# A fused attention and MLP-mixer kernel: hand-set order on every engine, first-batch masks on TensorE, and the next batch's token mix inside the current channel mix

## The chip, the cores and the metric

One core of a Trainium2 chip. The time is the device time of one execution in microseconds (us). The span of a profile is about 2 us shorter than the time of the same run (257.0 against 258.93 us before the change).

Engine names in the profile lines: PE is TensorE's matmul stream, PEld its weight loads, DVE is VectorE, ACT ScalarE, POOL GpSimd, SP SyncE. PSUM is the memory that the matmuls write to; its tiles are named after what they hold: ps_tr transposes of q and k, ps_s scores, ps_o attention output, ps_h `tok1`, ps_u `tok2`, ps_ut transposes of u, ps_v `ch1`, ps_w `ch2`. qb, kb and va are q, k and v cast to bf16, pT the exponentials, x_b the output of attention, u_sb the u of the reference.

## The reference, cut to what matters

```python
q, k, v: (4, 8, 768, 64)            # batch, heads, sequence, head dim; f32
keep = (key < 4) | (0 <= query - key < 128)        # 4 sink keys and a window of 128
x = softmax(where(keep, q @ k.T / 8, -1e9)) @ v    # heads joined: (4, 768, 512)
h = relu(x.T @ w_tok1) @ w_tok2                    # token mix, 768 -> 256 -> 768
u = x + h.T
out = u + relu(u @ w_ch1) @ w_ch2                  # channel mix, 512 -> 1536 -> 512
```

## The kernel before

The work is cut into eight groups of four heads, two groups for each batch. Per group: cast q and k to bf16 and transpose them (`tr`, six 128x128 TensorE transposes each), scores in three units per head pair (`sc`), exponential by ScalarE, masks, products with v (`pv`), normalisation by VectorE. Then per batch: `tok1` twice (once for each group), `tok2` and `utr` (I call `tok2` and `utr` together the *head*), then `ch1` and `ch2`. Attention of the next batch is laid into the channel mix of the current one.

```python
def sc(j, u):                        # cut
    ...
    nc.scalar.activation(pT[:, :, 512*u:512*u+n], ps[:, :, 0:n], AF.Exp, scale=scale)
    if u == 0:
        (nc.vector if fast else nc.gpsimd).tensor_tensor(... mask0 ..., op=ALU.mult)
    if dve_mask: ...                 # group 1, second head pair: VectorE multiplies
    elif u == 2:
        for i in range(2):           # window edges by GpSimd, in place
            nc.gpsimd.affine_select(out=cur, in_=cur, ...)
            nc.gpsimd.affine_select(out=prv, in_=prv, ...)

def tok2(st):
    ps = ps_mx.tile([P, DM], FP32, name="ps_u", tag="mx")    # two buffers, shared with ch1, ch2
    ...
    nc.vector.tensor_tensor(out=u_sb[:, st], in0=ps, in1=x_b[:, st], op=ALU.add)

with tc.manual_schedule(engines={PE}):      # only TensorE in the written order;
    ...                                     # the scheduler orders the other engines
    for b in range(B):
        t1, m = mixers.pop(b)
        main, fill = t1[1] + m, []          # m starts with the head
        ...                                 # attention of b + 1 at 0.03 .. 0.96 of main
        main = main + mixers[b + 1][0][0]   # first tok1 of b + 1
        for f in spread(main, fill):
            f()
```

The softmax here doesn't subtract the row's maximum and nothing guards it: scores larger than these inputs give would overflow.

Of the kernel before, what the change touches and what calls it, by code (L numbers as in the profile page):

```python
# [13 lines left out]
PE = mybir.EngineType.PE  # L14
# [3 lines left out]
def kernel(  # L18
# [45 lines left out]
    maskm = singles.tile([P, 2, P], BF16, name="maskm")  # L64
    warm = singles.tile([P, 512], BF16, name="warm")
    hm = singles.tile([P, 2, 4], BF16, name="hm")
    dm = singles.tile([4 * GH, GH, 1], FP32, name="dm")
    ks = [[singles.tile([P, P], BF16, name=f"ks{a}{j}") for j in range(2)] for a in range(2)]
    vs_c = singles.tile([4 * GH, NG, D], FP32, name="vs_c")
# [13 lines left out]


    def load_qk(g, lo, hi, q32, k32):
        b, h0 = g // GB, GH * (g % GB)
        return [nc.sync.dma_start(
            out=dst[:, lo:hi].rearrange("p h t d -> p h (t d)"),
            in_=src[b, h0 + lo:h0 + hi].rearrange("h (p t) d -> p h (t d)", t=NT))
            for src, dst in ((q, q32), (k, k32))]  # L90

    def load_v(g, v32):
        b, h0 = g // GB, GH * (g % GB)
        return nc.sync.dma_start(out=v32.rearrange("p h t d -> p (h t) d"),
                                 in_=v[b, h0:h0 + GH].rearrange("h (t p) d -> p (h t) d", p=P))

    def stage_tiles():
        return (stage.tile([P, GH, NT, D], FP32, name="q32"),
                stage.tile([P, GH, NT, D], FP32, name="k32"),
                stage.tile([P, GH, NT, D], FP32, name="v32"))  # L100

    def load_group(g, *behind):
        t3 = stage_tiles()
        for d in load_qk(g, 0, GH, t3[0], t3[1]) + [load_v(g, t3[2])]:
            after(d, *behind)
        return t3

    def load_sinks():
        for h in range(GH):
            nc.sync.dma_start(  # L110
                out=vs_c[4 * h:4 * h + 4],
                in_=v.rearrange("b (a h) s d -> h s (b a) d", h=GH)[h, 0:4])

    def load_weights(behind):
        wt1 = moe_w_tok1.rearrange("(t p) n -> p t n", p=P)
        wt2 = moe_w_tok2.rearrange("(t p) n -> p t n", p=P)
        wc1 = moe_w_ch1.rearrange("(t p) n -> p t n", p=P)
        wc2 = moe_w_ch2.rearrange("(t p) n -> p t n", p=P)
        hf = DCH // 2
        after(nc.gpsimd.dma_start(out=w_tok1, in_=wt1), behind)  # L120
        nc.gpsimd.dma_start(out=w_tok2, in_=wt2)
        nc.gpsimd.dma_start(out=w_ch1[:, :, 0:hf], in_=wc1[:, :, 0:hf])
        d = nc.gpsimd.dma_start(out=w_ch1[:, :, hf:DCH], in_=wc1[:, :, hf:DCH])
        nc.gpsimd.dma_start(out=w_ch2[:, 0:NF // 2], in_=wc2[:, 0:NF // 2])
        nc.gpsimd.dma_start(out=w_ch2[:, NF // 2:NF], in_=wc2[:, NF // 2:NF])
        return d

    def build_constants():
        nc.vector.memset(warm, 0.0)
        make_identity(nc, ident)  # L130
        nc.vector.memset(mask0, 1.0)
        nc.gpsimd.affine_select(
            out=mask0[:, :, 0], in_=mask0[:, :, 0], compare_op=ALU.is_ge,
            fill=0.0, base=0, pattern=[[0, 2], [1, P]], channel_multiplier=-1)
        nc.gpsimd.affine_select(
            out=mask0[:, :, 1], in_=mask0[:, :, 1], compare_op=ALU.is_ge,
            fill=0.0, base=-1, pattern=[[0, 2], [-1, P]], channel_multiplier=1)
        nc.vector.tensor_copy(out=maskm, in_=mask0[:, 0])
        nc.vector.memset(mask0[0:4], 1.0)
        nc.vector.memset(hm, 1.0)  # L140
        nc.vector.memset(hm[64:128, 0], 0.0)
        nc.vector.memset(hm[0:64, 1], 0.0)
        for a in range(2):
            for j in range(2):
                nc.gpsimd.memset(ks[a][j], 0.0)
        nc.vector.memset(vsink, 0.0)

    def build_sinks():
        nc.gpsimd.memset(dm, 1.0)
        nc.gpsimd.affine_select(  # L150
            out=dm[:, :, 0], in_=dm[:, :, 0], compare_op=ALU.is_ge, fill=0.0,
            base=0, pattern=[[-4, GH]], channel_multiplier=1)
        nc.gpsimd.affine_select(
            out=dm[:, :, 0], in_=dm[:, :, 0], compare_op=ALU.is_ge, fill=0.0,
            base=3, pattern=[[4, GH]], channel_multiplier=-1)
        for h in range(GH):
            nc.vector.tensor_scalar(
                out=vsink[0:4 * GH, :, h, 0:D], in0=vs_c,
                scalar1=dm[:, h], scalar2=None, op0=ALU.mult)
            nc.vector.tensor_copy(  # L160
                out=vsink[0:4 * GH, :, h, D:D1],
                in_=dm[:, h:h + 1].to_broadcast([4 * GH, NG, 1]))


    class Group:
        pass

    def cast_tiles():
        G = Group()
        G.qb = bfp.tile([P, 2, NT, 2, D], BF16, name="qb")  # L170
        G.kb = bfp.tile([P, 2, NT, 2, D], BF16, name="kb")
        G.va = bfp.tile([P, GH, NT, D1], BF16, name="va")
        G.qT, G.kT, G.pT = [None, None], [None, None], [None, None]
        return G

    def cast_qk(G, j, q32, k32, fast):
        for (src, dst, eng) in ((q32, G.qb, nc.vector), (k32, G.kb, nc.gpsimd)):
            o = dst[:, j].rearrange("p t i d -> p i t d")
            (eng if fast else nc.gpsimd).tensor_copy(out=o, in_=src[:, 2 * j:2 * j + 2])

    def cast_v(G, v32):
        nc.gpsimd.memset(G.va[:, :, :, D:D1], 1.0)
        nc.gpsimd.tensor_copy(out=G.va[:, :, :, 0:D], in_=v32)

    def attention(g, G, x_b, fast):
# [3 lines left out]
        def tr(j, which):  # L189
# [4 lines left out]
            dst = att.tile([P, P, NT], BF16, name="qT" if which == 0 else "kT")  # L194
            view = ps.rearrange("d t p -> d p t")
            if which == 1 and not fast:
                nc.scalar.activation(dst, view, AF.Copy)  # L197
            else:
                nc.vector.tensor_copy(out=dst, in_=view)  # L199
            flat = dst.rearrange("d p t -> d (p t)")  # L200
            if which == 0:
                G.qT[j] = flat
            else:
                G.kT[j] = flat
                nc.gpsimd.tensor_tensor(  # L205
                    out=kz[j][:, 8 * j:8 * j + 8].rearrange("p (i s) -> p i s", i=2),
                    in0=flat[:, 0:4].unsqueeze(1).to_broadcast([P, 2, 4]), in1=hm, op=ALU.mult)

        def sc(j, u):
            dve_mask = g == 1 and j == 1  # L210
# [3 lines left out]
            n = 0  # L214
            for kt in (2 * u, 2 * u + 1):
                w = (2 if kt < NT - 1 else 1) * P
                for i in range(2):
                    nc.tensor.matmul(  # L218
                        ps[:, i, n:n + w],
                        G.kT[j][ds(64 * i, 64), ts(kt, P)], G.qT[j][ds(64 * i, 64), ds(kt * P, w)],  # L220
                        start=True, stop=True)
                n += w
            pT = G.pT[j]
            nc.scalar.activation(pT[:, :, 512 * u:512 * u + n], ps[:, :, 0:n], AF.Exp, scale=scale)  # L224
            if u == 0:
                (nc.vector if fast else nc.gpsimd).tensor_tensor(
                    out=pT[:, :, 0:2 * P], in0=pT[:, :, 0:2 * P],
                    in1=mask0.rearrange("p i c q -> p i (c q)"), op=ALU.mult)
            if dve_mask:
                lo, hi = (2 * P, 4 * P) if u == 0 else (512 * u, 512 * u + n)  # L230
                for x in range(lo, hi, 2 * P):
                    w = min(2 * P, hi - x)
                    nc.vector.tensor_tensor(
                        out=pT[:, :, x:x + w], in0=pT[:, :, x:x + w],
                        in1=maskm.rearrange("p c q -> p (c q)")[:, 0:w].unsqueeze(1).to_broadcast([P, 2, w]),
                        op=ALU.mult)
# [43 lines left out]
    def mixer(b, x_b):  # L280
# [53 lines left out]
        m = [T2(0), T2(1), X(0), T2(2), X(1)]  # L334
        m += [T2(3), X(2), C1(0, 0), T2(4), X(3), C1(0, 1), T2(5), X(4), C1(0, 2), C1(0, 3), X(5)]
        m += [C1(0, f) for f in range(4, NF)]
        for n in range(3):
            m += [C1(1, f) for f in range(4 * n, 4 * n + 4)] + [C2(n, p) for p in range(NF // 4)]
        m += [C2(s, p) for s in range(3, NT) for p in range(NF // 4)]
        return t1, m  # L340
# [16 lines left out]

    with tc.manual_schedule(engines={PE}):
        xs = [None] * B
        parts, mixers, held = {}, {}, {}  # L360
# [4 lines left out]

        def begin(g):
            t3 = held.pop(g)
            G = cast_tiles()
            for j in range(2):
                cast_qk(G, j, t3[0], t3[1], False)  # L370
            cast_v(G, t3[2])
            parts[g] = attention(g, G, xs[g // GB], False)
            if g + 2 < NG:
                held[g + 2] = load_group(g + 2)
# [6 lines left out]
        A, C = stage_tiles(), stage_tiles()  # L381
        load_qk(0, 0, 2, A[0], A[1])
        load_qk(0, 2, 4, A[0], A[1])
        load_qk(1, 0, 2, C[0], C[1])
        va0 = load_v(0, A[2])
        load_sinks()
# [89 lines left out]
```

## Time and profile before

| | before |
|---|---|
| median of 3 runs | 259.17 us (258.85 to 259.41) |
| span of the profile | 257.0 us |
| last output of batch 0's attention | 52 us |
| mean granted TensorE clock | 0.951 |

The page of the kernel before: busy time, and the span in 40 slices of 6.4 us each (tenths busy; for PEclk tenths of the full clock).

```profile
PE 212.4 (83%) x1678; PEld 122.3 (48%) x1704; DVE 92.5 (36%) x193; ACT 120.6 (47%) x205; POOL 98.2 (38%) x153
...
PE   6183470779989899887998999787989998999993
...
POOL 3469404970198483245764622026325400000000
PEclk9998555899999999999999999999999999999999
```

The first eight slices, 51 us, are a different regime from the rest: TensorE is busy 24 of the first 50 us, and its clock falls to half. In the windows view of the same stretch the columns are the stretch, its length, busy us of each engine with instruction counts, granted clock, DMA share and GB/s:

```profile
20.00:30.00 10.00, 2.99 (x25) 1.66 (x25) 7.29 (x13) 2.78 (x5) 8.58 (x16) 0.68 1.20 197
30.00:40.00 10.00, 5.83 (x61) 3.62 (x60) 6.23 (x19) 4.20 (x5) 0.00 (x0) 0.50 1.22 210
40.00:50.00 10.00, 3.90 (x39) 2.97 (x41) 1.49 (x6) 1.37 (x3) 7.45 (x12) 0.62 1.12 311
```

The chain that ended last in that stretch (start, length, what):

```profile
30.06 15.60 DMA k_232<-in_k_dram
45.70 0.08 issue
45.78 0.83 POOL kb L179
46.61 0.71 POOL pT L241
47.31 0.59 POOL pT L244
```

k_232 is group 2, of the next batch. GpSimd's timeline shows how it got into the chain (start, length, line, operation; in brackets the idle time before it and what ended it):

```profile
41.04 1.47 POOL L183 CAST va<-v_119 128x1536 bf16<-128x1536 f32 x1 [12.46 <-DMA v_119<-in_v_dram]
43.82 0.83 POOL L179 CAST qb<-q_231 128x768 bf16<-128x768 f32 x1 [1.31 <-DMA q_231<-in_q_dram]
...
45.78 0.83 POOL L179 CAST kb<-k_232 128x768 bf16<-128x768 f32 x1 [0.19 <-DMA k_232<-in_k_dram]
46.56 0.75 POOL L241 TENSOR_SCALAR_AFFINE_SELECT pT<-pT 128x640 bf16<-128x640 bf16 x1
```

GpSimd runs its instructions in order. It waits 12.46 us for v of group 1, then casts group 2, and only then masks group 1 at 46.56 us, which the last outputs of batch 0 wait for. After that, TensorE's own waits are small. These lines are from the waits view of the whole execution (who waited for whom, us in total, times, longest):

```profile
PE ps_s L218 <- ACT pT L224: 2.6, 4, 0.8
PE ps_ut L303 <- DVE u_sb L298: 2.4, 6, 0.5
...
PE ps_v L309 <- ACT uT L304: 2.1, 4, 0.7
PE ps_v L309 <- ACT v_1248 L311: 2.0, 3, 1.1
```

The same list has larger waits for GpSimd (8.6 and 4.1 us) and for kT (5.9 us), but all of them lie in the start. From 52 us on TensorE waits for ScalarE, and in the heads for VectorE.

### The profile page before, as it was taken

How to read it: one execution, taken by the hardware profiler on the slowest of the kernel's cores; microseconds unless marked ns; L12 is line 12 of the kernel's file. 1: busy time of each engine (PE TensorE's matmuls, PEld its weight loads, DVE VectorE, ACT ScalarE, POOL GpSimd, SP SyncE). 2: the span in 40 equal slices, each digit the busy share in tenths (PEclk: the TensorE clock that was granted, in tenths of full speed). 3: DMA queues.
4: the chain of work that ended last, by engine and by line, in shares of the span. 5: the costliest groups of instructions: out<-in, count | busy, mean ns of one | idle time of the engine just before them, and what ended most of it. 6: DMA issues, size and time to landing. Idle time of an engine off the chain costs nothing.

```text
span 257.0 us, 4162 instructions
## 1 busy us (share of the span) xinstructions
PE 212.4 (83%) x1678; PEld 122.3 (48%) x1704; DVE 92.5 (36%) x193; ACT 120.6 (47%) x205; POOL 98.2 (38%) x153
## 2 busy tenths in 40 slices
PE   6183470779989899887998999787989998999993
PEld 2051240546635455653554556454645565554441
DVE  4555960452212246560123354530222455201122
ACT  1054150237786830369865502488576104773300
POOL 3469404970198483245764622026325400000000
PEclk9998555899999999999999999999999999999999
DMA  6999999999934726600000122000011121001122
GB/s 175 315 215 203 190 210 305 320 344 275 279 122 163 248 82 168 188 14 3 0 25 18 41 84 82 3 0 0 3 42 45 42 82 43 0 0 43 41 82 82
DMA packets 40659, 29.40 MB, mean 114 GB/s; under 512 B 25664, under 2 KB 37696, under 8 KB 40640
## 3 DMA queue, kind: packets, MB, share of 16 engines
q1 hardware_dynamic: 36816, 25.07, 32.9%
q0 software_dynamic: 3680, 3.93, 9.3%
q8 instruction: 13, 0.21, 0.3%
q10 hardware_dynamic: 144, 0.13, 0.1%
q14 instruction: 6, 0.05, 0.1%
HBM read 26.77 MB, written 6.29 MB: 129 GB/s over the span
## 4 chain that ended last, share of the span: by engine, by line
PE 62%; ACT 15%; DMA 9%; DVE 8%; issue 2%; POOL 1%; SPq 1%; DVEq 0%; ACTq 0%; POOLq 0%
PE ps_w L318 23%; PE ps_v L309 19%; ACT pT L224 9%; DMA k_232<-in_k_dram 6%; PE ps_tr L193 4%; PE ps_h L290 3%; DMA q_117<-in_q_dram 3%; PE ps_s L218 3%; PE ps_u L297 2%; DVE u_sb L298 2%; PE ps_ut L303 2%; PE ps_o L262 2%; ACT uT L304 2%; PE ps_o L266 2%; ACT kT L197 1%
## 5 line engine op out<-in xcount | busy, mean ns | idle before, releaser
L309 PE MATMUL ps_v<-uT,w_ch_105 128*128 128x384 bf16 x384 | 71.8, 325 | 7.2 <-ACT uT L304 2.1
L224 ACT ACTIVATE pT<-ps_s 128x1024 bf16<-128x1024 f32 (+1 forms) x48 | 43.6, 964 | 29.6 <-PE ps_s L218 29.6
L309 PEld LDWEIGHTS <-w_ch_105 128*128 128x128 bf16 x384 | 35.5, 97 | 32.1 <-issue 13.1
L321 DVE TENSOR_TENSOR o<-ps_w,u_sb 128x512 f32<-128x512 f32 x24 | 16.6, 692 | 44.0 <-PE ps_w L318 44.0
L199 DVE COPY qT<-ps_tr 128x768 bf16<-128x768 bf16 x16 | 15.2, 952 | 46.4 <-PE ps_tr L193 46.4
L241 POOL TENSOR_SCALAR_AFFINE_SELECT pT<-pT 128x640 bf16<-128x640 bf16 x30 | 22.8, 762 | 21.6 <-ACT pT L224 21.6
L218 PE MATMUL ps_s<-qT,kT 64*128 64x256 bf16 x192 | 17.0, 292 | 8.7 <-DVE kT L199 5.9
L269 DVE RECIPROCAL rc<-ps_o 128x4 f32<-128x4 f32 x48 | 8.7, 180 | 41.8 <-PE ps_o L266 23.7
L298 DVE TENSOR_TENSOR u_sb<-ps_u,x_b 128x512 bf16<-128x512 f32 x24 | 15.9, 688 | 19.1 <-PE ps_u L297 18.9
L270 DVE TENSOR_TENSOR x_b<-ps_o,rc 128x256 bf16<-128x256 f32 x48 | 20.4, 424 | 1.7
L262 PE MATMUL ps_o<-va,pT 128*128 128x65 bf16 x192 | 18.6, 200 | 1.6 <-DVE kT L199 0.9
L290 PE MATMUL ps_h<-x_b,w_tok_103 128*128 128x256 bf16 x96 | 12.6, 289 | 8.8 <-POOL ks_100 L205 8.6
L304 ACT ACTIVATE uT<-ps_ut 128x512 bf16<-128x512 bf16 x24 | 14.4, 601 | 11.3 <-PE ps_ut L303 11.1
L244 POOL TENSOR_SCALAR_AFFINE_SELECT pT<-pT 128x512 bf16<-128x512 bf16 x30 | 19.1, 638 | 0.0
L262 PEld LDWEIGHTS <-pT 128*128 128x128 bf16 x192 | 15.5, 102 | 5.6 <-POOL pT L241 0.7
L318 PE MATMUL ps_w<-w_ch_106,v_113 128*128 128x512 bf16 x67 | 17.7, 379 | 0.3
L318 PE MATMUL ps_w<-w_ch_106,v_555 128*128 128x512 bf16 x67 | 16.9, 379 | 0.3 <-issue 0.2
L318 PE MATMUL ps_w<-w_ch_106,v_1248 128*128 128x512 bf16 x67 | 16.9, 379 | 0.3 <-issue 0.2
L311 ACT ACTIVATE v_1941<-ps_v 128x384 bf16<-128x384 f32 x24 | 11.8, 491 | 10.9 <-PE ps_v L309 10.8
L218 PEld LDWEIGHTS <-kT 64*128 64x128 bf16 x192 | 7.8, 99 | 18.3 <-issue 9.3
L266 PE MATMUL ps_o<-va,pT 128*128 128x65 bf16 x160 | 16.4, 200 | 0.0
L318 PE MATMUL ps_w<-w_ch_106,v_1941 128*128 128x512 bf16 x70 | 15.9, 379 | 0.1
(103 smaller groups left out, 275.6 us busy)
## 6 DMA issues: line engine op xcount, KB each, us to landing
out_dram<-o SPq DMA_DIRECT2D x23, 256.0 KB, 2.0
w_ch_105<-in_moe_w_ch_dram POOLq DMA_DIRECT2D x2, 768.0 KB, 12.6
w_ch_106<-in_moe_w_ch_dram POOLq DMA_DIRECT2D x2, 768.0 KB, 22.8
q_114<-in_q_dram SPq DMA_DIRECT2D x2, 384.0 KB
k_115<-in_k_dram SPq DMA_DIRECT2D x2, 384.0 KB, 6.6
q_117<-in_q_dram SPq DMA_DIRECT2D x2, 384.0 KB, 6.4
k_118<-in_k_dram SPq DMA_DIRECT2D x2, 384.0 KB, 7.6
v_116<-in_v_dram SPq DMA_DIRECT2D x1, 768.0 KB, 9.5
```

The lines of the kernel that those rows point to most:

```text
L218: nc.tensor.matmul(ps[:, i, n:n + w], G.kT[j][ds(64 * i, 64), ts(kt, P)], G.qT[j][ds(64 * i, 64), ds(kt * P, w)], start=True, stop=True)
L224: nc.scalar.activation(pT[:, :, 512 * u:512 * u + n], ps[:, :, 0:n], AF.Exp, scale=scale)
L241: nc.gpsimd.affine_select(out=cur, in_=cur, compare_op=ALU.is_ge, fill=0.0, base=0, pattern=[[0, NT - 1], [1, P]], channel_multiplier=-1)
L244: nc.gpsimd.affine_select(out=prv, in_=prv, compare_op=ALU.is_ge, fill=0.0, base=-1, pattern=[[0, NT - 2], [-1, P]], channel_multiplier=1)
L262: nc.tensor.matmul(ps[:, h], pT[:, i, ds(256 * qt, P)], G.va[:, h, qt], start=(qt < 2 and h == 0), stop=(h == GH - 1 and qt == 0), skip_gr ...
L266: nc.tensor.matmul(ps[:, h], pT[:, i, ds(256 * (qt - 1) + P, P)], G.va[:, h, qt - 1], start=False, stop=(h == GH - 1), skip_group_check=True)
L270: nc.vector.tensor_tensor(out=x_b[:, qt, c0:c0 + GH * D].rearrange("p (h d) -> p h d", h=GH), in0=ps[:, :, 0:D], in1=rc.to_broadcast([P, G ...
L290: nc.tensor.matmul(ps, w_tok1[:, t, ts(tt, P)], x_b[:, t, ds(a * GH * D, GH * D)], start=(t == 0), stop=(t == NT - 1))
L298: nc.vector.tensor_tensor(out=u_sb[:, st], in0=ps, in1=x_b[:, st], op=ALU.add)
L304: nc.scalar.activation(uT[:, :, ts(st, P)], ps, AF.Copy)
L309: nc.tensor.matmul(ps, w_ch1[:, c, ts(ft, P)], uT[:, c, ds(half * HS, HS)], start=(c == 0), stop=(c == NC - 1))
L318: nc.tensor.matmul(ps, v1[:, ft, ts(st, P)], w_ch2[:, ft], start=(ft == 0), stop=(ft == NF - 1))
```

## The change

Its intent: write the order of all engines by hand, so that nothing of group 2 stands before batch 0; take batch 0's masks off GpSimd and VectorE by adding -30000 in PSUM with a matmul; issue the weights later, behind group 1's loads; hide the head of the next batch in the current channel mix; move kT evacuations from ScalarE to VectorE. The core of the diff, with cuts marked:

```diff
+    def build_masks():              # mneg: 0 where kept, -30000 elsewhere
+        ...
         def sc(j, u):
+            if first:               # groups 0 and 1
+                for i in range(2):
+                    nc.tensor.matmul(ps[:, i, 0:n], ident, mneg[...][:, 0:n],
+                                     start=True, stop=False, skip_group_check=True)
             ...
             nc.scalar.activation(pT[...], ps[:, :, 0:n], AF.Exp, scale=scale)
+            if first:
+                return
-            dst = att.tile([P, P, NT], BF16, ...)
-            if which == 1 and not fast:
-                nc.scalar.activation(dst, view, AF.Copy)
+            (by_act if g == 0 and j == 0 and which else by_dve)(dst, ps)   # cut
-    with tc.manual_schedule(engines={PE}):
+    with tc.manual_schedule():
+        load_k(G0, 0, 2, nc.scalar)          # three of the first k loads on a second queue
         ...
+        seq += [C(G1, 1, 0, by_pool), C(G1, 1, 1, by_pool), load_tok, lambda: cast_v(G1)]
+        seq += [lambda: load_ch1(0), lambda: hold.append(load_ch1(1))]
         ...
+        seq += [build_mask0, lambda: fetch(2, hold[0]), lambda: load_ch2(0), lambda: load_ch2(1)]
         ...
-                lo = 0.3 if b == 0 else 0.03            # attention at lo .. 0.96 of main
+                order += [step(h, 2, 0)] + [f for f, _ in nt1[0]]
+                order += [step(h, 3, i) for i in range(NT)] + [f for f, _ in nt1[1]]
+                lo, mid = (0.35, 0.76) if b == 0 else (0.02, 0.68)
+                ...                                     # attention and both tok1 at lo .. mid
+                hi = mid + 0.03                         # next batch's head at hi .. 0.97
```

GpSimd's part of a group's start is one block:

```python
def begin(g):
    G = held.pop(g)
    parts[g] = attention(g, G, xs[g // GB], False)
    for j in range(2):
        cast(G, j, 0, by_pool)       # q
        cast(G, j, 1, by_pool)       # k
    cast_v(G)                        # GpSimd too
    fetch(g + 2)
```

## The prediction

> **What bounds the kernel now.** Until about 52 us (batch 0's attention) TensorE mostly waits: the windows view shows it busy 2.99 of 10 us at 20:30 and 3.90 at 40:50, with a granted clock of 0.68, 0.50 and 0.62 from 20 to 50. The longest piece of the chain of waits is 15.60 us, the DMA of k_232, group 2's. The timeline shows why: GpSimd casts group 2 (43.8 to 46.6 us) before it masks group 1 (46.6 to 49.2), and before that it waits 12.5 us for v_119, which landed 27.7 us after its issue, beside the weight loads (issued 11.7 to 18.9 us). From 52 us TensorE is the limit. In the chain, four ch1 matmuls take 0.65 us and four ch2 matmuls 0.86: the spacing of the Trainium skill's "TensorE: Matmul & The Clock Gate" (section Back-to-back issue gap: N/2.4 + 2.5 ns), so the trace agrees. Charging every matmul so (64-row pairs half), I estimate 172 us of issue work after 52 us, 29 us of gaps, and 4 us after the last matmul.
>
> **Those gaps.** About 2.4 us in each of four heads (token mix, transposes, first ch1: ps_ut waits for the u_sb add, ps_u for the ReLU), and 5 to 6.3 us in each stretch where attention is interleaved (ps_v and ps_s wait for ScalarE, 14.7 of 20 us busy at 120:140).
>
> **What changes.**
> 1. Start: GpSimd no longer meets group 2's casts early; weights are issued after group 1's loads. Masks cost 16 matmuls of 512 columns and 8 of 384, about 4.8 us of TensorE (estimate) where it has slack; twelve affine selects of about 0.7 us leave GpSimd. Loads on two queues let the first scores start near 9 us instead of 13. VectorE becomes the busiest: seven 0.95 us evacuations, twelve 0.6 us normalisations, memsets, sink casts: about 20 us. Batch 0's last attention output moves from 52 to about 32 us. Saves about 20 us.
> 2. Heads of batches 1 to 3 hide in the previous channel mix: saves about 7 us. Batch 0's stays.
> 3. Twelve kT evacuations (0.81 us) move from ScalarE to VectorE, but attention is packed into two thirds of the channel mix, so ScalarE stays dense: gain 1 to 2 us.
> 4. Given back: about 3 us in batch 0's channel mix, where groups 2 and 3 (loaded behind ch1, beside ch2) arrive about when TensorE's fixed order wants them.
>
> **Sum.** 32 + 172 + 2 (head of batch 0) + 15 (interleave) + 1.5 (last mix) + 3 (late loads) + 4 (tail) = 229.5 us of span; the run is 2 us longer: 231.5 us. Range 223 to 243.
>
> **What would show it.** First token-mix matmuls of batch 0's second half near 32 us; no wait of GpSimd for k of group 2 before batch 0's x_b is complete; granted clock above 0.9 after 10 us; no ps_ut<-u_sb waits for batches 1 to 3, the last batch being about 31 us of pure ch1/ch2; ps_v and ps_s waits on ScalarE still the largest TensorE gaps; some wait for groups 2 or 3 between 40 and 62 us.
>
> **What would make it wrong.** Every engine now runs in a fixed order, so one late DMA or VectorE wait holds up all behind it: the start could end at 38 us. Groups 2 and 3 could come later (up to 8 us). Packing could make ScalarE the limit in the interleave (up to 8 us). If the order fits well, waits could nearly vanish (222 us).
>
> Chances: faster by over 2% 0.96, within 2% 0.03, slower 0.01.

## The result, and the profile after

The ratios are the mean time of one kernel's runs over that of the other's runs of the same rounds, so they are not quite the ratios of the quoted medians. Executions over 1.5% slower than the fastest of the same kernel are left out of the means.

| | before | after |
|---|---|---|
| median | 259.29 us | 238.96 us (238.73 to 239.08, 4 runs) |
| ratio to before | | 0.9217 [0.9201, 0.9233] |
| predicted | | 231.5 us (223 to 243) |
| span of the profile | 257.0 us | 237.1 us |
| mean granted clock | 0.951 | 1.0 |

The page of the kernel after, the same lines:

```profile
PE 212.1 (89%) x1708; PEld 119.8 (51%) x1729; DVE 100.6 (42%) x221; ACT 114.1 (48%) x195; POOL 88.9 (37%) x124
...
PE   6797788976999999978999999978999999999993
...
POOL 3567400449989200079985000089950000000000
PEclk9999999999999999999999999999999999999999
```

And the windows, where the last one is new trouble:

```profile
10.00:20.00 10.00, 8.67 (x88) 3.84 (x87) 8.11 (x17) 7.71 (x9) 8.00 (x11) 1.00 1.06 213
20.00:30.00 10.00, 7.50 (x103) 5.03 (x104) 6.91 (x21) 4.23 (x6) 4.80 (x7) 1.00 1.17 195
30.00:40.00 10.00, 8.31 (x67) 4.90 (x67) 5.15 (x11) 4.68 (x9) 0.00 (x0) 1.00 1.16 218
40.00:50.00 10.00, 9.94 (x74) 6.17 (x73) 1.71 (x2) 6.83 (x15) 4.25 (x6) 1.00 1.17 287
50.00:60.00 10.00, 6.31 (x58) 3.40 (x58) 2.48 (x8) 7.71 (x12) 6.84 (x9) 1.00 1.09 290
```

To see where the time went I cut both traces at matmuls that exist in each: the first matmul of batch 0's second `tok1` half, then the first `ch1` matmul of each batch, read from the timelines. Lengths in us:

| stage | before | after |
|---|---|---|
| start | 51.4 | 30.4 |
| head of batch 0 | 6.2 | 6.1 |
| from batch 0's first ch1 to batch 1's | 53.9 | 57.4 |
| to batch 2's | 54.1 | 53.0 |
| to batch 3's | 53.3 | 53.0 |
| to the end | 38.2 | 37.1 |

The stages differ in content. In the old layout two `tok2` and three `utr` of batches 1 to 3 (2 x 0.432 + 3 x 0.222 = 1.5 us by the kernel's own costs) come after the batch's first `ch1`, in the new one before it. And the first twelve transposes of the attention that follows (0.7 us at N/2.4 + 2.5 ns each) stand before that `ch1` in the old layout, after it in the new one. Corrected for both, batch 0's stage lost 2.7 us (57.4 - 1.5 - 53.9 + 0.7), the next two gained 1.1 and 1.0, and the end lost 0.4. **The start gained 21 us; everything after it lost 1 us, though hiding three heads was meant to gain about 7 us there.** That is the question for the experiments.

What TensorE waits for after the change, in the waits view:

```profile
PE ps_tr L193 <- POOL qb L116: 4.6, 3, 1.8
...
PE ps_s L219 <- ACT pT L225: 3.1, 6, 1.0
...
PE ps_w L313 <- DVE o L316: 1.6, 5, 0.4
...
PE ps_ut L298 <- DVE u_sb L293: 0.4, 1, 0.4
```

Of the waits of ps_ut for u_sb only batch 0's is left, as intended. In their place stand two that the kernel before did not have after its start: transposes waiting for GpSimd's casts, once for each of three batches, and ch2's accumulators waiting for VectorE's output add. The chain in batch 0's mix shows the first of the two:

```profile
54.88 0.75 POOL pT L236
55.63 0.59 POOL pT L239
56.22 0.70 POOL pT L236
56.92 0.59 POOL pT L239
57.51 1.12 POOL pT L229
58.63 0.77 POOL qb L116
59.40 0.77 POOL kb L116
```

For 3.75 us GpSimd masks group 2 (L236, L239, L229), and the casts of group 3 (L116) stand behind that in the written order. The Trainium skill's "TensorE: Matmul & The Clock Gate" (the table at its head) calls GpSimd's queue strict FIFO; this chain agrees.

### The profile page after: what moved, and what is told of

Same layout as the page of the kernel before. It is cut to its first block, busy times and chain, and to the rows that moved or that the text cites. A ratio compares the mean times of both kernels' runs of the same rounds, so it can differ in the third digit from the quotient of the medians.

```text
span 237.1 us, 4195 instructions
## 1 busy us (share of the span) xinstructions
PE 212.1 (89%) x1708; PEld 119.8 (51%) x1729; DVE 100.6 (42%) x221; ACT 114.1 (48%) x195; POOL 88.9 (37%) x124
## 4 chain that ended last, share of the span: by engine, by line
PE 68%; POOL 10%; DVE 9%; ACT 6%; DMA 3%; issue 2%; ACTq 0%; POOLq 0%
PE ps_w L313 26%; PE ps_v L304 20%; DVE o L316 5%; ACT pT L225 5%; PE ps_h L285 3%; PE ps_tr L193 3%; PE ps_u L292 3%; DMA k_113<-in_k_dram 3%; PE ps_s L219 3%; POOL pT L236 2%; PE ps_ut L298 2%; PE ps_o L257 2%; PE ps_o L253 2%; DVE x_b L265 2%; POOL pT L239 2%
## 5 line engine op out<-in xcount | busy, mean ns | idle before, releaser
L304 PE MATMUL ps_v<-uT,w_ch_103 128*128 128x384 bf16 x384 | 74.3, 325 | 1.4 <-ACT uT L299 0.7
L304 PEld LDWEIGHTS <-w_ch_103 128*128 128x128 bf16 x384 | 34.7, 97 | 25.0 <-issue 6.8
L229 POOL TENSOR_TENSOR pT<-pT,mask_92 128x512 bf16<-128x512 bf16 x12 | 13.8, 1154 | 52.2 <-ACT pT L225 52.2
L299 ACT ACTIVATE uT<-ps_ut 128x512 bf16<-128x512 bf16 x24 | 14.0, 596 | 32.6 <-PE ps_ut L298 32.5
L236 POOL TENSOR_SCALAR_AFFINE_SELECT pT<-pT 128x640 bf16<-128x640 bf16 x24 | 18.0, 752 | 5.5 <-ACT pT L225 5.5
L219 PE MATMUL ps_s<-qT,kT 64*128 64x256 bf16 x192 | 15.5, 263 | 4.6 <-ACT pT L225 3.1
L313 PE MATMUL ps_w<-w_ch_104,v_581 128*128 128x512 bf16 x69 | 18.1, 379 | 0.8 <-DVE o L316 0.6
L313 PE MATMUL ps_w<-w_ch_104,v_1338 128*128 128x512 bf16 x69 | 18.1, 379 | 0.8 <-DVE o L316 0.6
L313 PE MATMUL ps_w<-w_ch_104,v_111 128*128 128x512 bf16 x67 | 17.9, 379 | 0.8 <-DVE o L316 0.3
L306 ACT ACTIVATE v_1338<-ps_v 128x384 bf16<-128x384 f32 x24 | 11.9, 506 | 12.5 <-PE ps_v L304 12.5
L306 ACT ACTIVATE v_581<-ps_v 128x384 bf16<-128x384 f32 x24 | 11.9, 506 | 12.6 <-PE ps_v L304 12.6
L257 PE MATMUL ps_o<-va,pT 128*128 128x65 bf16 x192 | 17.3, 194 | 0.2
L306 ACT ACTIVATE v_2035<-ps_v 128x384 bf16<-128x384 f32 x24 | 11.8, 491 | 11.3 <-PE ps_v L304 11.2
L257 PEld LDWEIGHTS <-pT 128*128 128x128 bf16 x192 | 14.5, 98 | 3.5 <-issue 0.4
L306 ACT ACTIVATE v_111<-ps_v 128x384 bf16<-128x384 f32 x24 | 11.8, 495 | 9.0 <-PE ps_v L304 8.8
L313 PE MATMUL ps_w<-w_ch_104,v_2035 128*128 128x512 bf16 x70 | 15.9, 379 | 0.1
```

Source lines behind the costliest of these rows:

```text
L219: nc.tensor.matmul(ps[:, i, at:at + w], G.kT[j][ds(64 * i, 64), ts(kt, P)], G.qT[j][ds(64 * i, 64), ds(kt * P, w)], start=not first, stop= ...
L236: nc.gpsimd.affine_select(out=cur, in_=cur, compare_op=ALU.is_ge, fill=0.0, base=0, pattern=[[0, NT - 1], [1, P]], channel_multiplier=-1)
L257: nc.tensor.matmul(ps[:, h], pT[:, i, ds(256 * qt, P)], G.va[:, h, qt], start=(qt < 2 and h == 0), stop=(h == GH - 1 and qt == 0), skip_gr ...
L299: nc.scalar.activation(uT[:, :, ts(st, P)], ps, AF.Copy)
L304: nc.tensor.matmul(ps, w_ch1[:, c, ts(ft, P)], uT[:, c, ds(half * HS, HS)], start=(c == 0), stop=(c == NC - 1))
L306: nc.scalar.activation(v1[:, ft, ds(half * HS, HS)], ps, AF.Relu)
```

## The experiments

Each is the changed kernel with one edit, unless said otherwise. The changed kernel was not run again; the intervals of the ratios are 0.4 to 1.4 us to either side, and a difference of about 1 us is within them.

### 1. Masks of batch 0 back on VectorE and GpSimd

```diff
-            if first:                       # mask matmuls
-            if first:
-                return
+            if u == 0: (nc.vector if first else nc.gpsimd).tensor_tensor(... mask0 ...)
+            if dve_mask: ...                # as before the change
+            elif u == 2: ...                # affine selects
```

> The changed kernel with batch 0's masks multiplied and selected by VectorE and GpSimd again, as before the change, all in the hand-set order. Theory (the masks themselves were on the path of the start): twelve affine selects of 0.7 us and nine VectorE multiplies of 0.4 us come back into engines with fixed order, the last x_b of batch 0 moves from 31.3 to 34 to 37 us, total 242 to 245. Rival (the order and the later weights made the gain, the masks were incidental): within 1 us of 239, start ends at 31 to 32 us.

Measured: 252.91 us, ratio 0.9755 [0.9712, 0.9797]; the start ended at 44.7 us instead of 30.4. The masks were on the path, and more than twice as costly as the theory had said (14 us against 3 to 6). GpSimd's timeline:

```profile
14.22 0.75 POOL L244 TENSOR_SCALAR_AFFINE_SELECT pT<-pT 128x640 bf16<-128x640 bf16 x1 [4.62 <-ACT pT L226]
...
17.01 0.82 POOL L116 CAST qb<-q 128x768 bf16<-128x768 f32 x1
```

The selects wait 4.62 us for the exponentials, and the cast that stands behind them, of data that landed at 9.05 us, waits with them. The weight loads that GpSimd issues are late too (first one at 28.6 us against 17.7). The granted clock was 0.50 in all three windows from 10 to 40 us. Without any masks (run 4 below), and also with a slow clock, the start ended at 32.5 us; so some 12 of the 14 us come with the multiplies and selects in this order, a longer slow clock included, and about 2 with the absence of the mask matmuls.

### 2. Only TensorE in hand-set order

```diff
-    with tc.manual_schedule():
+    with tc.manual_schedule(engines={mybir.EngineType.PE}):
```

> The changed kernel with only TensorE in hand-set order, the other engines in the scheduler's order as before the change. Theory (the hand-set order of GpSimd and VectorE is most of the gain): the scheduler again lets casts of later groups or weight loads in early, start ends at 40 us or later, total 248 or more. Rival (the new program, with weights issued late and the masks on TensorE, is enough in any order): total within 2 us of 239.

Measured: 240.39 us, ratio 0.9266 [0.9227, 0.9304]. The rival is right: the hand-set order of the other four engines is worth about 1.4 us, and the intervals of the two ratios just overlap. It helps the start (34.6 us in the scheduler's order against 30.4; TensorE waits 3.6 us there for VectorE to prepare the mask tile mneg) and goes with a loss later (51.8 us against 53.0 in each of the two later attention stages, where in the scheduler's order no wait for GpSimd's casts is left).

### 3. Old masks and the scheduler's order: the fourth corner

Edits 1 and 2 together.

> Batch 0's masks by VectorE and GpSimd, and only TensorE in hand-set order: the fourth corner of masks by order. So far the start ended at 30.4 us (masks on TensorE, all hand-set), 34.6 (TensorE masks, scheduler's order), 44.7 (old masks, hand-set). Theory A (GpSimd's selects are bad because they stand in a fixed order ahead of casts; the scheduler would slip the casts in between): start ends at 36 to 40 us, total 241 to 246. Theory B (the selects themselves, on an engine that also casts and issues the weights, are the load): start ends at 43 us or later, total 248 to 255, whatever the order.

Measured: 243.94 us, ratio 0.9411 [0.9370, 0.9453]; start 39.1 us. Theory A holds. The four corners, end of the start and total:

| | masks on TensorE | masks on VectorE and GpSimd |
|---|---|---|
| all engines hand-set | 30.4 us, 238.96 | 44.7 us, 252.91 |
| only TensorE hand-set | 34.6 us, 240.39 | 39.1 us, 243.94 |

The two parts are not additive. With the old masks the hand-set order is 9 us slower than the scheduler's; with the new ones it is 1.4 us faster.

### 4. No masks at all in batch 0 (wrong result)

```diff
-            if first:
-                for i in range(2):
-                    nc.tensor.matmul(ps[:, i, 0:n], ident, mneg[...], ...)
+            # scores alone: start=True, stop=True
```

> Wrong result on purpose: batch 0's masks are left out altogether (no mask matmuls, no selects), all else as changed. The mask matmuls are 4.8 us of full-rate TensorE by estimate. Theory (TensorE has slack in the start; loads, casts and VectorE bound it): start ends at 29 to 30.4 us, total 237.5 to 239. Rival (they lie on the path, as chains of masks, scores and exponential): start ends at 25.5 to 27 us, total 234 to 235.5.

Measured: 240.32 us, ratio 0.9254 [0.9223, 0.9285], and wrong. Taking 4.8 us of matmuls away gained nothing; the total lies above the theory's range and far from the rival's. The runs fall in two pairs, 239.53 and 239.78, 240.87 and 240.94; the profile is of a run of the slower pair, and its start took 32.5 us, 2 us longer than with the masks. Its windows, where the changed kernel has a clock of 1.00 in both (shown above):

```profile
10.00:20.00 10.00, 8.11 (x72) 4.37 (x71) 7.85 (x15) 7.82 (x9) 7.80 (x11) 0.50 1.00 208
20.00:30.00 10.00, 8.56 (x77) 5.30 (x74) 5.85 (x16) 4.22 (x6) 4.80 (x7) 0.56 1.15 193
```

The Trainium skill's "TensorE: Matmul & The Clock Gate", Part 1, says that the slow clock is the default and that activity releases it. The mask matmuls fill gaps that TensorE had anyway, and with them the mean granted clock of the four runs is 0.996 to 1.0; without them it is 0.970 in the faster pair and 0.957 in the slower. That the clock, and nothing else, makes the slower pair slower was not tested by itself.

### 5. Weights issued early

```diff
+        seq[8:8] = [weights]        # tok, ch1, ch2, behind GpSimd's first cast (9.2 us)
-        ... load_tok, load_ch1, load_ch2 at their later places
```

> The changed kernel with all weight loads issued by GpSimd behind the first casts (about 10 us), as early as before the change, nothing else moved. Theory (the late weights are a second large part of the start's gain): v of group 1 lands at 35 to 41 us instead of 19.4, its cast blocks GpSimd's queue, the start (to the second token-mix half) ends at 40 to 47 us instead of 30.4, total 246 to 254. Rival (with the masks on TensorE the start no longer cares): start ends before 33 us, total within 2 us of 239, and batch 0's channel mix may even gain from earlier groups 2 and 3.

Measured: 255.13 us, ratio 0.9838 [0.9811, 0.9866]; the start ended at 45.8 us. The theory holds. v of group 1 landed at 39.49 us instead of 19.42, in the waits view:

```profile
POOL va L182 <- DMA v<-in_v_dram: 16.3, 2, 15.8
...
PE ps_o L257 <- POOL va L182: 9.3, 1, 9.3
```

The Trainium skill's "Trainium Kernel Development and Optimization" (Key Constraints) says that loads issued from different engines share the same DMA engines and interleave. Here GpSimd's weights held back SyncE's v by 20 us. Batch 0's channel mix stayed at 57.4 us although groups 2 and 3 had more time: v of group 3 landed 2 us after that stage began, in the changed kernel 21 us after. So it is not these loads that make the stage 57.4 us long.

### 6. Heads at the start of their own channel mix

```diff
+                if b > 0: main = head + main          # and lo, mid scaled to keep attention's place
-                fill += [... nhead ...]               # heads no longer in the mix before
```

> The changed kernel, but the heads of batches 1 to 3 (second token product, transposes) stand at the start of their own channel mix instead of inside the one before; attention keeps its place. Theory A (hiding a head is worth its idle time of 2.3 us each): plus 6 to 8 us, 245 to 247. Theory B (hidden heads cost about as much as they save, since ps_u and ps_w share two PSUM buffers, about 1.2 us of ps_w waits per batch): plus 2.5 to 4.5 us, 241.5 to 243.5, and the ps_w waits on DVE o fall below 0.5 us per batch.

Measured: 241.07 us, ratio 0.9289 [0.9250, 0.9328], 2.1 us more than with hidden heads, where I had predicted that hiding saves about 7. Theory B is nearer (a little below its range). The wait of ps_w for VectorE is no longer in the list of waits; ps_ut's for u_sb is back (1.5 us in four waits), and ps_u now waits for the output add (1.1 us in three). My reading is that hiding a head removes its gaps and the shared PSUM buffers give a large part back; run 10 tests the second half.

### 7. The old arrangement behind the new start

```diff
+                main = t1[1] + head + main            # b > 0; head mixed with ch1 as before
-                lo, mid = (0.35, 0.76) if b == 0 else (0.02, 0.68)
+                lo, mid = (0.35, 0.96) if b == 0 else (0.03, 0.96)
+                main = main + nt1[0]
```

> The changed start with the arrangement of before from there on: heads at the start of their channel mix, attention spread over 0.03 to 0.96 of it (0.35 to 0.96 in batch 0). The ledger of the two traces says that after the start the change gained nothing in sum (gaps of 28.6 us before, 28.5 after). If that holds: 237 to 240. If hiding the heads is a true gain that something in the start paid for: 244 to 247.

Measured: 237.97 us, ratio 0.9187 [0.9135, 0.9239], start 30.4 us. So the ledger holds: the rearrangement after the start gained nothing. It may have cost a microsecond, but the two intervals overlap. It is 3.1 us faster than run 6, in which the heads are not hidden either but the attention is still packed. By stages that gain lies in batch 0's mix: 54.1 us here, about 55 with the contents made equal as above, against 58.4. The next two take 54.0 and 53.3 us (54.0 made equal) against 53.6 each. So packing cost time in batch 0's mix and not in the later ones. The run also lays the heads among `ch1` and moves `tok1`, so packing was not tested by itself.

### 8. Casts of the second group ahead of the first group's masks

```diff
-                order = [lambda g=g: begin(g)]
+                order = [lambda g=g: begin(g)] + ([lambda h=h: begin(h)] if b > 0 else [])
-                ..., lambda h=h: begin(h),
+                ..., (lambda h=h: begin(h)) if b == 0 else (),
```

> The changed kernel with the casts of the second group of batches 2 and 3 put right behind those of the first group in GpSimd's order, ahead of the first group's masks. Theory (the hand-set GpSimd order, casts behind masks, makes the transposes wait 1.57 us in each of the two stages): ps_tr waits below 0.3 us there, each stage 51.7 to 52.2 us instead of 53.0, total 236.5 to 237.5. Rival (ScalarE's exponentials bound these stretches): the wait reappears at ps_s or ps_v, total within 0.7 us of 239.

Measured: 238.97 us, ratio 0.9220 [0.9193, 0.9248]; no gain. The two waits that it aimed at did go (the one left is batch 0's), but others came up:

```profile
PE ps_tr L193 <- POOL qb L116: 1.8, 1, 1.8
...
PE ps_tr L193 <- DVE ks L202: 1.1, 4, 0.4
...
PE ps_h L285 <- ACT h L287: 0.9, 2, 0.5
```

The edit also shifted every later piece of attention by one place, so this run does not say whether the order of the casts or the shift made the new waits. The total lies in the rival's range, but the new waits are not the ps_s and ps_v that it named. I count it as inconclusive.

### 9. Casts of second groups by VectorE

```diff
-                cast(G, j, 0, by_pool)
-                cast(G, j, 1, by_pool)
+                cast(G, j, 0, by_dve if g % GB else by_pool)
+                cast(G, j, 1, by_dve if g % GB else by_pool)
```

> The changed kernel with the q and k casts of every second group from batch 1 on by VectorE instead of GpSimd. Theory (GpSimd's fixed order is the wait in all three stages): ps_tr waits of second groups vanish in batch 0's channel mix too, 1.3 us less in each later stage and 2 to 3 us less in the first, total 233.5 to 235.5. Rival (batch 0's channel mix waits for the loads of groups 2 and 3): the later stages gain the same, the first stays within 0.7 us of 57.4, total 236 to 237.

Measured: 234.23 us, ratio 0.9040 [0.9012, 0.9068]: 4.7 us less, within the theory's range and not the rival's. The wait of ps_tr for GpSimd's q casts (4.6 us before) has left the list, the two later stages take 51.8 us and batch 0's 55.3 instead of 57.4. So 2.1 us of what looked like late loads was GpSimd's queue. Group 3's casts show it, first in the changed kernel, then in this run:

```profile
58.57 0.82 POOL L116 CAST qb<-q_568 128x768 bf16<-128x768 f32 x1
```

```profile
52.65 0.56 DVE L113 CAST qb<-q 128x768 bf16<-128x768 f32 x1 [0.24 <-DMA q<-in_q_dram]
54.84 1.07 DVE L113 CAST kb<-k 128x768 bf16<-128x768 f32 x1 [1.64 <-DMA k<-in_k_dram]
```

On VectorE the first starts 5.9 us earlier, and now the casts do wait for loads. Whether GpSimd would have done as well in another order is what run 8 left open.

### 10. ps_u from the other PSUM pool

```diff
-            ps = ps_mx.tile([P, DM], FP32, name="ps_u", tag="mx")
+            ps = (ps_mx if b == 0 else ps_ms).tile([P, DM], FP32, name="ps_u",
+                                                   tag="mx" if b == 0 else "ms")
```

> The changed kernel with ps_u of batches 1 to 3 taken from the other PSUM pool (that of the transposes), so that it no longer shares two buffers with ps_w. Theory (sharing made ps_w wait for VectorE's output add, 1.2 to 1.8 us per batch): ps_w waits below 0.5 us per stage, total 235.5 to 237. Rival (the wait only moves to ps_ut and ps_u, which then share two buffers): total within 1 us of 239.

Measured: 235.87 us, ratio 0.9098 [0.9077, 0.9119]: 3.1 us less, 0.9 us in batch 0's stage and 1.0 in each of the next two. The theory holds; ps_w's wait for VectorE left the list, and no wait of ps_ut or ps_u for each other came in its place.

### 11. Both together

```diff
(edits 9 and 10)
```

> Both gains together: q and k casts of second groups by VectorE, ps_u of batches 1 to 3 from the transposes' PSUM pool. They removed different waits (ps_tr on GpSimd: minus 4.7 us; ps_w on VectorE: minus 3.1 us). If they add: 231 to 232. If one wait hid the other: 233 to 234.5.

Measured: 231.50 us, ratio 0.8919 [0.8897, 0.8941], correct. The gains add: 7.5 us under the changed kernel, so this version beats both. Its stages are 30.3, 6.2, 54.5, 50.8, 50.8 and 37.1 us. The windows of its batch 0 mix, beside the 6.31 us of the changed kernel at 50:60:

```profile
50.00:60.00 10.00, 8.26 (x76) 4.71 (x74) 7.29 (x14) 8.09 (x13) 7.07 (x9) 1.00 1.08 294
60.00:70.00 10.00, 9.73 (x109) 5.80 (x109) 6.44 (x20) 6.85 (x10) 9.35 (x13) 1.00 1.19 306
```

### 12. Score units spread singly

```diff
+                order += [step(g,1,0), step(g,1,1), begin(h), step(g,1,2), step(h,0,0), step(g,1,3), ...]
+                for n in range(6): order += [step(h, 1, n), step(g, 3, n)]     # cut; on top of run 11
-    ... name="att", bufs=3
+    ... name="att", bufs=4
```

> As the combination, with the score blocks spread singly between the second group's transposes and the first group's value products, instead of in pairs, and four buffers for qT and kT. Theory (the remaining 2.5 us of ps_s and 1.5 us of ps_v waits per stage come from two exponentials in a row on ScalarE in front of the ReLUs): 1.5 to 2.5 us less per stage, 225 to 228 in all. Rival (ScalarE is simply dense there, pairs or not): within 1.5 us of the combination.

Measured: 235.44 us (234.52 to 236.88), ratio 0.9072 [0.9029, 0.9116], 3.9 us slower than run 11 and less steady. My theory fell, and not even the rival's range held. In the later stages the two are about equal (51.1 and 51.0 us against 50.8): charged at N/2.4 + 2.5 ns per matmul, as in the prediction, and counted from 50 ns up, the gaps before ps_s shrank from 2.5 to 1.8 us and those before ps_v grew from 1.5 to 2.0. The loss is in batch 0: its mix took 57.3 us against 54.5, with 3.1 us of gaps before ps_o against 0.6. Here part of it is a wait that run 11 does not list:

```profile
PE ps_o L257 <- POOL pT L229: 1.3, 1, 1.3
```

The head of batch 0 was 0.9 us longer in this profile as well, in code that both share; there the clock was 0.83 at 30:40.

## Why the prediction was right, and where it was off

The time, 238.96 us, lies within 223 to 243, but 7.5 us above the 231.5 that I had named: the start came out as forecast, and the stretch after it 8 us longer.

**The start: right, with an incomplete reason.** I predicted 52 to 32 us; it went to 31.3 by the same mark (the second batch of token-mix matmuls behind the last output). Both named causes were needed in the hand-set order: with the old masks the start ends at 44.7 us, with early weights at 45.8. What the loads on two queues are worth was not tested by itself (the first scores start at 7.8 us instead of 13.0; I had said 9). I had put the masks down as matmuls "where it has slack", which fits run 4. What I had not seen is that the clock falls without them (run 4), and that the hand-set order pays only together with them (run 3).

**Heads: wrong in worth.** The step "Heads of batches 1 to 3 hide in the previous channel mix: saves about 7 us" failed. The ps_ut waits went, as said, but run 6 puts the gain at 2.1 us: ps_u inside the channel mix competes with ps_w for two PSUM buffers, which run 10 shows by taking ps_u out of them (3.1 us).

**Interleave and late loads: the mis-sized terms.** The sum had "15 (interleave) + 3 (late loads)". In the whole stretch after the start I predicted 229.5 - 32 = 197.5 us; before it was 257.0 - 52.2 = 204.8 and it became 237.1 - 31.3 = 205.8. So all of the miss is here. Charged as in the prediction, TensorE's gaps in the three stretches with attention are 10.0, 7.0 and 7.0 us in the trace after, 24 us (some 3 of them missing records, see below) where the two terms allowed 18. The 3 us for late loads looks right only by chance: batch 0's stretch is indeed 2.9 us longer than the next (57.4 - 1.5 against 53.0), but earlier loads did not shorten it (run 5) and GpSimd's queue was 2.1 us of it (run 9). I had warned of packing, but of ScalarE as its limit. The runs show GpSimd's order in its place (4.6 us of transposes waiting for casts; run 9 gets 4.7 us back) and the PSUM buffers (run 10 gets 3.1 back). The move of twelve kT evacuations to VectorE ("gain 1 to 2 us") was not tested by itself. That run 11 lands at 231.50 us, the predicted number, is chance: the two repairs happen to equal the miss, and the remaining gaps were not predicted one by one.

**The marks.** Second half of the token mix near 32 us: yes, 30.4 to 31.3. No wait of GpSimd for group 2's k before batch 0 was done: yes; it waits for group 2's q, which landed at 42.4 us, after batch 0's attention and with no mask of batch 0 behind it. Clock above 0.9 after 10 us: yes. No ps_ut waits for batches 1 to 3, last mix about 31 us: yes for the first, nearly for the second (from its first ch1 at 200.0 us to its last ch2 near 233 us). ScalarE's waits the largest gaps: no, the largest is ps_tr for GpSimd. Some wait for groups 2 or 3 between 40 and 62 us: TensorE waited 1.8 us for a cast of group 3, but the cast stood in GpSimd's queue and did not wait for its load (run 9).

**The accounting.** "172 us of issue work and 29 us of gaps" was a poor split. The trace of before has 67 to 70 of each batch's 72 ch2 matmuls, and a missing record is counted as a gap. In traces with all of them the later stages have 47.1 us of work and not 46.1. Stage lengths, which need no such charge, are the safer ledger.

**Open.** How much of batch 0's 54.5 us in run 11 is late loads, now that the casts do wait for them; whether run 8's order is good if nothing else is shifted.

## What to carry to other kernels

When all engines run in a written order, look at each in-order engine for work of one kind (casts for the next block) that stands behind work of another (masks that wait for an exponential), and move one of the two to another engine; a fixed order is only as good as its slowest neighbour, and an automatic order may already do better in the steady state. Before hiding a dependent stretch inside a longer one, count the accumulator buffers that the two would share. And cut the traces into stages by equal landmarks: a total of minus 20 us hid a part of the change that gained nothing.

## What the Trainium skill lacked or had wrong

- "TensorE: Matmul & The Clock Gate", Part 1, says that activity releases the slow clock, but not what share of its window has to be active. Here TensorE counted as 81% and 86% busy in two 10 us windows at a clock of 0.50 and 0.56 (run 4), and as 87% and 75% in the same two windows of the changed kernel at 1.00. The busy share alone does not tell the states apart; a matmul also counts as busy for longer at the slow clock (a score matmul on average 387 ns against 264 in the first of these windows).
- The same page warns of idle gaps and advises warming up before a measurement; that extra matmuls laid into gaps in mid-kernel can cost nothing and go with a higher clock is on no page that I read. Taking 4.8 us of them away (estimate) gave 240.32 us instead of 238.96, and a mean clock of 0.957 to 0.970 instead of 0.996 to 1.0.
- "GPSIMD Engine Reference" puts VectorE at roughly 2 times GpSimd for ordinary elementwise arithmetic (opening), a factor that its engine selection table (section 4.1) keeps to operations with two inputs; for a cast, which has one, it has no time. The cast of 128x768 f32 to bf16 took 0.83 us on GpSimd in the kernel before, and on VectorE 0.56 us three times and 1.81 us once; in run 9 VectorE's took 0.84 (q, eight casts, two of them in the start) and 0.73 us (k, six) on average, so hardly less. The move paid because the casts started earlier, not because they were shorter.
- No page that I read treats the cost of a hand-set order against a scheduler's. Here it ranged from 1.4 us better to 9 us worse with one other thing changed.
